# Retention and a squared-ReLU FFN on one core: which engine turns q and k for the later chunks

## The chip, the cores and the metric

The kernel runs on one core of a Trainium2 chip. Time is device time in microseconds from the first to the last instruction of that core; the times of a kernel are from several runs, and the profile is of one execution. Engines are named as in the profile: PE is TensorE (matmul), PEld its weight loads, DVE is VectorE, ACT is ScalarE, POOL is GpSimd, SP is SyncE, which here starts the DMA transfers.

## The reference

A retention layer (attention without softmax, with a decay for each head) feeds a feed-forward network. Shapes: q, k and v are 8 batches x 8 heads x 576 positions x 64; the FFN sees 4608 tokens of width 512, with a hidden width of 2048. All data are float32.

```python
scores = scale * np.matmul(q, k.transpose(0, 1, 3, 2))
Dmat = np.where(rel >= 0, gamma[:, None, None] ** rel[None, :, :], 0.0)
x = np.matmul(scores * Dmat, v)            # then heads side by side: 4608 x 512
h = np.maximum(x @ w_in, 0.0)
out = h * h @ w_out
```

What matters here: the scores contract over the 64 channels of a head, so TensorE needs q and k with the channels on the partitions. They arrive with the positions on the partitions. So each chunk of q and k has to be turned first.

## The kernel before

**Tiling.** The positions of each batch are cut into chunks of 128, the fifth of a batch having 64: 40 chunks, 8 of them short (numbers 4, 9, 14, ..., 39). The tokens are also cut into 9 blocks of 512 for the FFN. Both FFN products are done in a Strassen-like scheme with seven block products in place of eight (`PRODUCTS`), whose sums and differences are made by VectorE.

**First stage, to about 540 us.** A loop over i from 0 to 40 (`N_CH`) does chunk i's scores and finishes chunk i-1, and between these pieces works off FFN steps of earlier blocks. The order is written out by hand; each engine executes its own instructions strictly as listed, and semaphores tie the engines together. One round of the loop, for i above 4, is:

- `retain_a(i-1)`: products within the second half of the chunk (L457) and the growth of the state `u` (L460), then a ScalarE copy of the state (L466);
- `turn(i)` for i below `N_TURN` = 9;
- `move(C, i)`: the copies still open for chunk i;
- `ffn(i-1, 0)`: some FFN steps (`ffn_in`, L616), two or three in most rounds, by the schedule `PACE`; ahead of each step up to three open copies (`move(3)`);
- `retain_b(i-1)`: products with the state (L492), and a ScalarE copy of two columns (L495) that the next products wait for;
- `scores(i)`: the score matmuls (L435), then VectorE multiplies by the mask (L443);
- `retain_c(i-1)`: products within the first half, and the copy out to the FFN's input (L514);
- `spread(i+1)` and `flip(i+2)` for chunks from 9 on, then `ffn(i-1, 1)`, then the loads of later chunks.

**Two ways to turn a chunk.** `turn` uses TensorE: 16 transposes of 64 rows (8 for a short chunk) against an identity (L414) into PSUM, then ScalarE copies out k (L417) and VectorE q (L418). The tile they write in PSUM (`ps_t`, one buffer) is the one that the scores use as well. `flip` uses VectorE: two instructions (L392) that transpose 32x32 blocks of k and of q. The blocks then still lie in the wrong partitions, and `spread` lists 16 copies (8 for a short chunk) that bring them to their places; ScalarE makes these copies (L403, in `move`), a few at a time between the FFN steps.

**An FFN step** is four matmuls (eight records in the profile, L616) into one of three PSUM buffers (h_a, h_b, h_c), and what takes the result out: ScalarE for the first and fourth of the seven products (L626, L632), VectorE for the others (L628, L630, L635, L639, L642), VectorE again for the squares (L623) and for the sums that go to DRAM (L554 to L557). From block 3 on (earlier for a few steps) each step also brings a piece of the second weight's conversion: L210 to L228 and the sums L245 to L248 on VectorE, L218 and L219 on ScalarE.

**Second stage, from about 600 us.** The second FFN product (L903) with all its operands prepared; neither `turn` nor `flip` has a part in it.

**Buffers that matter.** q has three load buffers, k five, v four; the tile for turned q and k has three; the flipped tile two.

Of the kernel before, what the change touches and what calls it, by code (L numbers as in the profile page):

```python
# [40 lines left out]
def kernel(  # L41
# [50 lines left out]
    N_CH = len(chunks)  # L92
# [192 lines left out]
    def fetch_raw(count):  # L285

        for _ in range(count):
            if n_raw[0] < min(N_W1, n_made[0] + N_RAW):
                fetch_w(n_raw[0])
                n_raw[0] += 1  # L290
# [25 lines left out]
    def convert(count):  # L316
        for _ in range(count):
            f = next(w_in_steps, None)
            f and f()
# [52 lines left out]
    def scale_q(i, engine):  # L372
        ci, cs = chunks[i][1], chunks[i][3]
        t = loaded[i][0][:cs]
        engine.tensor_tensor(t, t, dv[:cs, :, NCH + ci:NCH + ci + 1].to_broadcast([cs, H, D]), op=ALU.mult)  # L375
# [1 line left out]

    N_TURN = 9  # L380
    moves = []

    def new_qk(i):
# [16 lines left out]
    def move(count, i=N_CH):  # L400

        while moves and count and moves[0][0] <= i:
            nc.scalar.copy(*moves.pop(0)[1:])  # L403
            count -= 1
# [63 lines left out]
    def retain_a(i):  # L468

        b_, ci, c0, cs = chunks[i]  # L470
        xp[0] = ps_x.tile([128, 2, 256], F32, tag="x", name="x_ps", padded_shape=[128, 2, 512])
        clean.clear()
        if ci == 0:
            u_ps[0] = ps_u.tile([128, HP, D], F32, tag="u", name="u_ps")
        if cs < C:
            return
        own, grow = within(i, 1)
        for j in range(0, len(own), 2):
            for f in own[j:j + 2] + grow[j:j + 2]:
                f()  # L480
        grown(i, 0)

    def retain_b(i):

        s = st[i]
        b_, ci, c0, cs = chunks[i]
        for h in reversed(range(cs // CH)):
            if 2 * ci + h == 0:
                continue
            u = u_sb[(2 * ci + h) % 3]  # L490
            for hp, e, b in HEADS[0:2] + HEADS[4:6] + HEADS[2:4] + HEADS[6:8]:
                nc.tensor.matmul(x_at(hp, b, h), lhsT=u[rows(e), hp, :], rhs=s["qT"][rows(e), hp, CH * h:CH * h + CH],  # L492
                                 start=clears(b, hp // 2), stop=False, skip_group_check=True)

        nc.scalar.copy(u_sb[(2 * ci + (cs // CH)) % 3][:, 0:2, 0:1], xp[0][:, :, cs - CH:cs - CH + 1])  # L495

    def retain_c(i):

        b_, ci, c0, cs = chunks[i]
        own, grow = within(i, 0)  # L500
        more = ci + 1 < NCH
        for j in range(0, len(own), 2):
            for f in own[j:j + 2] + (grow[j:j + 2] if more else []):
                f()
        tok = b_ * S + c0
        at = tok
        p = xp[0][:, :, 0:256].rearrange("p a (g t) -> p a g t", g=2)
        while at < tok + cs:
            n = at // TOK

            while steps and steps[0][0] <= (n - 2 if n > 4 else n - 3):
                step()
            end = min(tok + cs, (n + 1) * TOK)
            nc.scalar.copy(xT[n][:, :, at - n * TOK:end - n * TOK].rearrange("p (a g) t -> p a g t", a=2),  # L514
                           p[:, :, :, at - tok:end - tok])
            if more and at == tok:
                grown(i, 1)
            at = end
            if n_next[0] < N_BLK and (n_next[0] + 1) * TOK <= at:
                steps.extend(block_steps(n_next[0]))  # L520
                n_next[0] += 1
        st[i] = loaded[i] = None
# [47 lines left out]
    def first_in(j, halves=(0, 1)):  # L570

        assert n_made[0] > j
        wi, m, e = pieces[j]
        mp, mm = divmod(m, 2)
        p = ps_f.tile([128, 2, HT], F32, tag="f", name="h_ps")
        w = w_in[mp][:, mm, 2 * e:2 * e + 2, :, :].rearrange("p s c f -> p (s c) f")
        lo, hi = halves[0], halves[-1] + 1
        p = p[:, lo:hi, :]
        for c in range(N_DM):
            nc.tensor.matmul(p.rearrange("p h t -> p (h t)"), lhsT=w[:, c, :], rhs=xT[0][:, c, lo * HT:hi * HT],  # L580
                             start=(c == 0), stop=(c == N_DM - 1))

        t = g_room[mp % 2][:, 3:7:3, mm, :] if e else g_room[mp % 2][:, 0:5:4, mm, :]
        t = t[:, lo:hi, :]
        nc.scalar.activation(t, p, AF.Relu)

        some(2)
        queue.append(lambda: nc.vector.tensor_tensor(t, t, t, op=ALU.mult))
        if mm and e and hi == 2:
            queue.append(lambda: [nc.sync.dma_start(  # L590
                g_dram[0, a:b, :, 2 * mp:2 * mp + 2, :].rearrange("s p m t -> p s (m t)"),
                g_room[mp % 2][:, a:b, :, :].rearrange("p s m t -> p s (m t)")) for a, b in QUARTERS])
        if j >= N_W1 - 4:

            sums_w.setdefault(0, sum_w_in(0)).pop(0)()
            if n_next[0] > 1:
                if 1 not in sums_x:
                    sums_x[1] = sum_x(1)
                sums_x[1].pop(0)()
# [80 lines left out]
    def step():  # L680
        n, f, *args = steps.pop(0)
        done[0] += 1
        f(*args)
# [43 lines left out]
    def warm(count, wide):  # L727
        t = ps_f.tile([128, 512], F32, tag="f", name="idle_ps")
        for _ in range(count):
            if wide:  # L730
                nc.tensor.matmul(t[:, 0:128], lhsT=idle, rhs=idle, start=True, stop=True)
            else:
                for b in range(2):
                    nc.tensor.matmul(t[rows(b), 0:64], lhsT=idle[rows(0), rows(b)], rhs=idle[rows(0), 0:64], start=True, stop=True,
                                     skip_group_check=True)
# [4 lines left out]
    for i in range(N_CH + 1):  # L740
        if i <= N_EARLY:

            if i == 1:
                convert(2)
            elif i == 2:
                convert(5)
            if i >= 1:
                retain_a(i - 1)
                if i < 3:
                    warm(4, False)  # L750
                else:
                    convert(1)
                    first_in(2 * i - 5, (0,))
                    convert(5)
                retain_b(i - 1)
                if i < 3:
                    warm(4, False)
                retain_c(i - 1)
            convert((0, 1, 1, 0, 1)[i])
            if i == N_EARLY:  # L760
                fetch_raw(2)
                step()
            scores(i)
            if i == 2:
                convert(5)
                first_in(0, (0,))
            elif i == 3:
                convert(1)
                first_in(2, (0,))
                convert(5)  # L770
            elif i == N_EARLY:
                convert(5)
                step()
                convert(6)
            scale_q(i + 1, nc.gpsimd)
            if i < N_EARLY:
                if i < 2:
                    warm(6, False)
                turn(i + 1)
        else:  # L780
            if i == N_EARLY + 1:
                gone[0] = TOK
            retain_a(i - 1)
            if i < N_TURN:
                turn(i)
            move(C, i)
            ffn(i - 1, 0)
            retain_b(i - 1)
            if i < N_CH:
                scores(i)  # L790
            retain_c(i - 1)
            if N_TURN <= i + 1 < N_CH:
                spread(i + 1)
            if N_TURN <= i + 2 < N_CH:
                flip(i + 2)
            ffn(i - 1, 1)
        if i == 0:
            fetch_raw(2)
        if i < N_TURN - 1:
            load(i + 3)  # L800
        else:
            if i == N_TURN - 1:
                load(i + 3, "qk")
            if i + 4 < N_CH:
                load(i + 4, "qk")
            if i + 3 < N_CH:
                load(i + 3, "v")
        if 0 < i < N_EARLY:
            fetch_raw(1)
        if i > N_EARLY:  # L810
            for j in range(i + 1 + 2 * (i > N_EARLY + 1), min(i + 4, N_CH)):
                scale_q(j, nc.gpsimd)
# [233 lines left out]
```

## Time and profile before

| | before |
|---|---|
| time, median of 3 runs | 997.35 us (994.88 to 998.98) |
| profiled execution | 996.09 us, span 994.4 us, mean granted TensorE clock 0.993 |
| TensorE busy from 225 to 545 us | 305.9 of 320 us |
| VectorE busy from 225 to 545 us | 286.9 of 320 us |
| ScalarE busy from 225 to 545 us | 186.5 of 320 us |
| copies L403, whole run | 440, 177.0 us busy, 402 ns each |
| flips L392, long chunks, whole run | 24 of k at 699 ns, 24 of q at 665 ns |
| transposes L414, whole run | 68 of k, 68 of q, chunks 0 to 8 |

The busy shares of an engine tell which is fullest, not what the others cost. To see that, one looks at the times when the fullest engine waits, and at what it waits for: the profile lists for each wait the engine and line that ended it. A row of the list of waits reads "who, which tile, which line <- whom it waited for: microseconds in total, times, the longest". The granted clock has to be read beside the busy time: a matmul at half the clock counts as busy for twice as long.

### The profile page before, as it was taken

How to read it: one execution, taken by the hardware profiler on the slowest of the kernel's cores; microseconds unless marked ns; L12 is line 12 of the kernel's file. 1: busy time of each engine (PE TensorE's matmuls, PEld its weight loads, DVE VectorE, ACT ScalarE, POOL GpSimd, SP SyncE). 2: the span in 40 equal slices, each digit the busy share in tenths (PEclk: the TensorE clock that was granted, in tenths of full speed). 3: DMA queues.
4: the chain of work that ended last, by engine and by line, in shares of the span. 5: the costliest groups of instructions: out<-in, count | busy, mean ns of one | idle time of the engine just before them, and what ended most of it. 6: DMA issues, size and time to landing. Idle time of an engine off the chain costs nothing. (4 is left out here: it accounts for less than half of the span.)

```text
span 994.4 us, 24115 instructions
## 1 busy us (share of the span) xinstructions
PE 960.5 (97%) x10092; PEld 855.8 (86%) x10092; DVE 788.7 (79%) x1458; ACT 350.2 (35%) x871; POOL 131.9 (13%) x121
## 2 busy tenths in 40 slices
PE   7899999999999989989999999999999999999998
PEld 6655777888878778877788889999999999999998
DVE  4789798768889899998986777777777677777766
ACT  3445575765665756746651000000000000000000
POOL 3211222212223231312211000000000000000000
PEclk9999999999999999989999999999999999999999
DMA  8884657655697589769358999684673757556351
GB/s 199 245 239 114 184 171 207 191 146 181 204 303 231 172 251 257 218 185 301 109 200 303 402 401 336 233 280 174 234 263 141 274 191 269 192 218 215 125 212 44
DMA packets 185037, 219.19 MB, mean 220 GB/s; under 512 B 118624, under 2 KB 135008, under 8 KB 175968
## 3 DMA queue, kind: packets, MB, share of 16 engines
q1 hardware_dynamic: 182816, 217.13, 67.3%
q8 instruction: 79, 1.29, 0.5%
q10 hardware_dynamic: 2112, 0.52, 0.2%
q14 instruction: 30, 0.25, 0.1%
HBM read 128.23 MB, written 89.39 MB: 219 GB/s over the span
## 5 line engine op out<-in xcount | busy, mean ns | idle before, releaser
L616 PE MATMUL h_b<-room,w 128*128 128x256 f32 x736 | 181.9, 391 | 10.6 <-DVE room L635 4.3
L403 ACT COPY qk<-flip 32x256 f32<-32x256 f32 x440 | 177.0, 402 | 6.3
L616 PEld LDWEIGHTS h_b<-room,w 128*128 128x128 f32 x736 | 139.9, 193 | 33.2 <-DVE room L635 6.1
L903 PE MATMUL o_b<-w,room 128*128 128x128 f32 x1168 | 144.5, 275 | 0.7 <-DVE room L854 0.7
L903 PEld LDWEIGHTS o_b<-w,room 128*128 128x128 f32 x1168 | 137.2, 192 | 0.9 <-DVE room L854 0.9
L903 PE MATMUL o_c<-w,room 128*128 128x128 f32 x1008 | 123.0, 275 | 0.0
L903 PEld LDWEIGHTS o_c<-w,room 128*128 128x128 f32 x1008 | 117.7, 192 | 0.0
L616 PE MATMUL h_c<-room,w 128*128 128x256 f32 x480 | 115.9, 385 | 0.0
L917 ACT COPY r<-o_a 128x128 f32<-128x128 f32 x53 | 14.1, 266 | 272.5 <-PE o_a L903 241.9
L616 PE MATMUL h_a<-room,w 128*128 128x256 f32 x448 | 107.6, 383 | 0.0
L616 PEld LDWEIGHTS h_c<-room,w 128*128 128x128 f32 x480 | 91.9, 193 | 13.6 <-DVE room L642 0.3
L616 PEld LDWEIGHTS h_a<-room,w 128*128 128x128 f32 x448 | 83.7, 190 | 12.1 <-ACT room L626 0.3
L633 POOL TENSOR_TENSOR room<-room 128x512 f32<-128x512 f32 x32 | 36.9, 1152 | 370.4 <-ACT room L632 264.5
L903 PE MATMUL o_a<-w,a 128*128 128x128 f32 x688 | 85.6, 275 | 0.0
L903 PEld LDWEIGHTS o_a<-w,a 128*128 128x128 f32 x688 | 81.2, 192 | 0.1
L623 DVE SCALAR_TENSOR_TENSOR room<-room 128x512 f32<-128x512 f32 x96 | 72.3, 753 | 3.3
L580 PE MATMUL h_ps<-room,w 128*128 128x512 f32 (+1 forms) x160 | 58.7, 515 | 3.3 <-DVE w L228 2.5
L375 POOL TENSOR_TENSOR q_ld<-q_ld,dv 128x512 f32<-128x512 f32 (+1 forms) x39 | 48.6, 1245 | 76.7 <-DMA q_ld<-in_q_dram 50.6
L457 PEld LDWEIGHTS x_ps<-qk,v_ld 64*64 64x64 f32 x1152 | 40.3, 136 | 17.8 <-issue 11.8
L457 PE MATMUL x_ps<-qk,v_ld 64*64 64x64 f32 x1152 | 49.7, 226 | 5.0 <-ACT u_sb L495 4.0
L580 PEld LDWEIGHTS h_ps<-room,w 128*128 128x128 f32 x160 | 29.2, 190 | 25.0 <-issue 20.4
L445 POOL TENSOR_TENSOR v_ld<-v_ld,dv 128x512 f32<-128x512 f32 (+1 forms) x40 | 47.5, 1187 | 13.6 <-DMA v_ld<-in_v_dram 5.9
(111 smaller groups left out, 1392.6 us busy)
## 6 DMA issues: line engine op xcount, KB each, us to landing
g_dram<-room SPq DMA_DIRECT2D x32, 1792.0 KB, 7.7
a<-g_dram SPq DMA_DIRECT2D x43, 1024.0 KB, 7.0
room<-g_dram SPq DMA_DIRECT2D x20, 1024.0 KB, 6.6
w<-w_dram SPq DMA_DIRECT2D x7, 1792.0 KB, 13.2
out_dram<-room SPq DMA_DIRECT2D x17, 512.0 KB, 3.2
w<-in_moe_w_in_dram SPq DMA_DIRECT2D x16, 512.0 KB, 5.6
w<-in_moe_w_out_dram SPq DMA_DIRECT2D x16, 512.0 KB, 3.9
v_ld<-in_v_dram SPq DMA_DIRECT2D x31, 256.0 KB, 4.4
```

What stands on the lines that cost most here:

```text
L375: engine.tensor_tensor(t, t, dv[:cs, :, NCH + ci:NCH + ci + 1].to_broadcast([cs, H, D]), op=ALU.mult)
L403: nc.scalar.copy(*moves.pop(0)[1:])
L445: nc.gpsimd.tensor_tensor(vs[:cs], vs[:cs], dv[:cs, :, ci:ci + 1].to_broadcast([cs, H, D]), op=ALU.mult)
L457: own.append(lambda hp=hp, e=e, b=b: nc.tensor.matmul(x_at(hp, b, h), lhsT=s["vs"][rows(h), 2 * hp + b, :], rhs=s["ret"][rows(h), e, hp, : ...
L580: nc.tensor.matmul(p.rearrange("p h t -> p (h t)"), lhsT=w[:, c, :], rhs=xT[0][:, c, lo * HT:hi * HT], start=(c == 0), stop=(c == N_DM - 1))
L616: nc.tensor.matmul(p[:, mm, :], lhsT=w[:, c, :], rhs=xs[n][right][:, c, :], start=(j in OPENS and mm == 0 and c == 0), stop=(j in CLOSES a ...
L623: nc.vector.scalar_tensor_tensor(t, t, 0.0, t, op0=ALU.max, op1=ALU.mult)
L633: nc.gpsimd.tensor_tensor(g["A11"], g["A11"], g["A11"], op=ALU.mult)
L903: nc.tensor.matmul(p, lhsT=s["lefts"][left][:, m, :], rhs=w_out[j][:, m, WO_SLOT[right], :], start=(i in OPENS and m == 0), stop=(i in CLO ...
L917: nc.scalar.copy(r[:, 0, 0:128], p)
```

## The change

For chunks 19 to 39 TensorE turns q and k again, as it does for chunks 0 to 8; only chunks 9 to 18 keep the way over VectorE and ScalarE. It is meant for the part of the run in which VectorE has the second weight to convert beside the FFN.

```diff
-    N_TURN = 9
+    N_TURN, N_BACK = 9, 19
...
             retain_a(i - 1)
-            if i < N_TURN:
+            if i < N_TURN or N_BACK <= i < N_CH:
                 turn(i)
             move(C, i)
             ffn(i - 1, 0)
...
             retain_c(i - 1)
-            if N_TURN <= i + 1 < N_CH:
+            if N_TURN <= i + 1 < N_BACK:
                 spread(i + 1)
-            if N_TURN <= i + 2 < N_CH:
+            if N_TURN <= i + 2 < N_BACK:
                 flip(i + 2)
             ffn(i - 1, 1)
```

The loads, and the order of the instructions on SyncE and GpSimd, stay as they are.

## The prediction

> **What bounds the kernel now.** I read first the busy shares and the 40 slices of the page, then the busy time of each engine in stretches of 10 us, then the list of who waited for whom on TensorE from 225 to 541 us, then the order of time around the longest of these waits. The busy shares say that TensorE (97%) is the engine that sets the time and that VectorE (79%) and ScalarE (35%) are not:
>
> ```profile
> PE 960.5 (97%) x10092; PEld 855.8 (86%) x10092; DVE 788.7 (79%) x1458; ACT 350.2 (35%) x871; POOL 131.9 (13%) x121
> PEclk9999999999999999989999999999999999999999
> ```
>
> The average hides the stage that the change touches: chunks 19 to 39, from the first flip that goes (210.9 us) to the last scores (528 us). There the other two are nearly as full. Columns of the stretches: from and to, length, then busy us of PE, PEld, DVE, ACT and POOL with instruction counts, granted clock, DMA share, GB/s:
>
> ```profile
> 245.00:255.00 10.00, 9.19 (x94) 7.65 (x94) 9.90 (x18) 6.59 (x16) 0.47 (x1) 1.00 0.42 105
> 255.00:265.00 10.00, 10.00 (x77) 8.23 (x73) 7.45 (x13) 6.30 (x16) 3.84 (x4) 0.83 0.90 281
> ...
> 315.00:325.00 10.00, 8.53 (x90) 7.08 (x86) 9.15 (x16) 9.06 (x21) 3.68 (x4) 1.00 0.95 265
> ...
> 425.00:435.00 10.00, 6.52 (x50) 5.05 (x49) 9.96 (x15) 3.85 (x10) 3.60 (x3) 0.73 0.06 25
> ```
>
> Read the last row: TensorE worked 6.5 of 10 us, at a mean clock of 0.73, while VectorE worked all ten. So TensorE is the bound, but in a few places it stands still for VectorE or ScalarE. All its waits from 225 to 541 us (columns: total us, times, longest):
>
> ```profile
> PE sc_ps L435 <- ACT qk L403: 3.5, 6, 1.1
> PE h_b L616 <- DVE room L628: 3.5, 1, 3.5
> PE x_ps L457 <- ACT u_sb L495: 2.8, 3, 2.1
> PE h_b L616 <- DVE room L635: 2.6, 2, 1.3
> PE h_b L616 <- DVE room L541: 1.6, 1, 1.6
> ```
>
> That is 14.0 us. Two more losses don't show as waits. First, three times a set of score matmuls that takes 0.65 us elsewhere is stretched (252.55 to 254.57, 322.91 to 325.85, 464.47 to 466.93 us, 7.4 us in place of 1.95): 5.5 us, of which 3.5 are in the list, so 1.9 more. Second, the granted clock falls to 0.50 after such places: the stretches at 255, 425, 435 and 495 us show 0.83, 0.73, 0.93 and 0.83, that is 1.7 + 2.7 + 0.7 + 1.7 = 6.8 us, less 0.6 that fell into the wait itself: 6.2 us. All told about **22 us** of TensorE's time in this stage are lost, and every one of these waits is for an instruction of VectorE or ScalarE.
>
> **What the skill says.** "TensorE: Matmul & The Clock Gate", Part 1 (the HAM clock gate): after a window of about 3.4 us with too little activity the clock is halved, and it comes back after a busy window. The trace agrees: 0.50 from about 430 to 436.6 us, behind a wait of 3.48 us, and about 3.4 us at half clock behind the stretched scores at 253 us. Part 4 of the page (PE-mode transpose) says that a transpose does not count as activity there. No run so far tells; but in the early stage, where TensorE already turns q and k, the clock is 1.00 from 0 to 100 us. "PSUM — Partial Sum Buffer", Terms, says that two engines must not be on one bank and quadrant at once. It bears on the two copies out of the turned chunk, which share their banks; in the program order the VectorE copy (L418) waits for the ScalarE copy (L417), and the trace has that wait: 4.8 us in 3 times.
>
> **The change part by part.** 21 chunks move: 16 of 128 rows, and 5 of 64 rows (19, 24, 29, 34, 39).
>
> (a) Removed from ScalarE: 16x16 + 5x8 = 296 copies (L403). The trace has just these 296 between 225 and 541 us, 119.1 us at 402 ns. Added: 21 copies L417, 16 of 585 ns and 5 of 372 ns, 11.2 us. ScalarE is lighter by 108 us. Its time is worth only what TensorE waited for: the three stretched scores (5.5 us), and the clock dip behind the first (1.7 us).
>
> (b) Removed from VectorE: 21 pairs of L392, 16x(699+665) + 5x(693+659) ns = 28.6 us. Added: 21 copies L418, 16x685 + 5x419 ns = 13.1 us. VectorE is lighter by 15.5 us, 0.68 us a chunk.
>
> (c) Added on TensorE: 16 transposes for a long chunk, 8 for a short one. The early turns price it in place: x8 and x8 from 62.42 to the next work at 63.06, and a short chunk, x4 and x4, from 34.44 to 35.08, 0.64 us each, since the two halves of a long chunk run beside one another:
>
> ```profile
> 62.42 0.46 PE L414 MATMUL t_ps<-w,k_ld 64*128 64x64 f32 x8
> 62.72 0.41 PE L414 MATMUL t_ps<-w,q_ld 64*128 64x64 f32 x8
> 63.06 3.70 PE L580 MATMUL h_ps<-room,w 128*128 128x512 f32 x8
> ```
>
> 21 x 0.64 = **13.4 us**, all on the engine that sets the end. By the mean durations (257 and 245 ns, start included) with no overlap of halves it could be up to about 20 us (9.1 us busy for the 136 early ones, 67 ns each, times 296 = 19.8); I take 13.4, since those sums hold the start of the kernel.
>
> (d) The waits for VectorE (7.7 us: 1.60, 1.28, 1.29 and 3.48). In each the VectorE has been full for some 10 us (9.9 of 10), so work taken from it there shortens the wait: 0.68 us a chunk net, and TensorE, coming 0.64 us later because it transposes, would wait that much less. That is 1.3 us for each: 1.3 + 1.28 + 1.29 gone. In the run-up to the longest the flips at 425.5 and 426.1 us go (1.28 with their overlap) and no added copy stands between, so 1.9 of 3.48: 5.8 us in all. The dip behind it (2.8 us) I count half, since 1.6 us of wait beside small matmuls may still trigger it: 1.4.
>
> (e) The wait for L495 (2.14 of its 2.8 us at 496.8 us). ScalarE had finished its copies and stood in L218, which waited for VectorE (L210, 1.01 us). So it is VectorE's lateness again; 0.68 + 0.64 = 1.3 us goes, with ScalarE free of copies also in the short ones 0.6: 2.0, and its dip, 1.7.
>
> (f) New waits. L418 must be through before the scores. Ahead of it on VectorE stand only evacuations of the earlier FFN steps; behind it the evacuations of the half chunk's FFN steps, for whose banks TensorE could wait. Between turn and scores TensorE has two or three FFN steps of 1.73 us and 0.4 to 0.7 us of L492, about 5 to 6 us. VectorE's lag, read as the time from the end of the scores to the start of L443, is 0 to 4.1 us and once 5.6 (chunk 32). L443 has the same room on the other side of the scores and was waited for 0.8 us in the whole run. So I cost L418 at nothing, hidden behind these steps. Early on TensorE did wait for it, 2.4 us in 2 times; there only one FFN step lies between.
>
> (g) Loads of q. Three buffers turn around at the transposes in place of the flips, two chunks later. The q load of chunk i+4 is then held until turn(i+1), soon after it is reached; the queue was held there anyway by L558, which waited 148 us for VectorE between 200 and 620 us. The data are needed two chunks (of some 14 us) later than for the flip, against 5.7 us for a landing. Nothing.
>
> The sum: 13.4 - (5.5 + 1.7 + 5.8 + 1.4 + 2.0 + 1.7) = 13.4 - 18.1 = -4.7 us. It reaches the end: from 540 to 600 us TensorE is 100% busy and from 530 on it waits 1.1 us in all. 997.35 - 4.7 = **992.6**.
>
> **The rivals.** *Everything comes back*: with both engines lighter all 22.1 us go: 13.4 - 22.1 = -8.7, 988.6 us. For it: all losses hang on the two relieved engines. Against: VectorE still works 0.85 of this stage (286.9 of 320 us from 225 us on, less 15.5). *TensorE pays, VectorE stays late*: the bursts of weight work (L245 to L248 and slow two-operand adds of 1.2 to 1.5 us at 351 and 416 us) make the waits, not the flips; then only ScalarE's 7.2 us come back: +6.2, 1003.5 us. For it: TensorE is the fullest engine and gets the work. *The copy takes the place of the wait*: L418 waits for L417 and holds up VectorE, and TensorE waits as it did early, 1.2 us at each of half the chunks, 13 us, on top of -4.7: +8, 1005.6 us, slower. Against it: the room in (f).
>
> **How the numbers follow.** Forecast 0.60, spread 989.5 to 996, half of it beyond 0.5% (992.4); everything back 0.16; TensorE pays 0.16; the copy 0.08. Faster 0.46, same 0.30, slower 0.24. The range takes in the floor, 988, and reaches up to the third case, 1003.
>
> **What would show it.** The waits of scores for L403 after 225 us are gone; L414 costs 0.64 us a chunk; TensorE's idle time from 225 to 541 us falls from 14 to about 4 us and the clock in the 10 us stretches stays at 1.00 but for one or so; ScalarE loses 108 us, VectorE 15.5. It is wrong if L435 waits for L418 or L417 at many chunks, if L628 and L635 keep their waits, if the transposes cost over 0.9 us in place, or if the clock falls at other places.

## The result and the profile after

The changed kernel takes 991.97 us (median of 4 runs, 991.45 to 993.54) against 996.61 us of the kernel before in the same job, that is, among runs of both taken together (994.88 to 998.98): a ratio of 0.9954, 95% interval 0.993 to 0.9979. In a later job it took 992.71 us against 996.19, a ratio of 0.9966 (0.9952 to 0.998). So it is 3.5 to 4.6 us faster.

The busy shares and the clock in the 40 slices, after:

```profile
PE 968.1 (98%) x10388; PEld 864.0 (87%) x10388; DVE 769.7 (78%) x1437; ACT 242.6 (24%) x596; POOL 126.9 (13%) x121
PEclk9999999999999999999999999999999999999999
```

TensorE is busier (7.6 us more), ScalarE has lost 107.6 us, VectorE 19.0. That TensorE's busy time rises by less than the 13.4 us of the transposes fits the clock: the 8 in the row of before is gone, and the same products take less time (before, an FFN step at half clock took 3.78 us at 431 us, one at full clock 1.89 us at 437 us). All waits of TensorE from 225 to 541 us, after (total us, times, longest):

```profile
PE x_ps L457 <- ACT u_sb L495: 1.4, 2, 1.0
PE h_b L616 <- DVE room L541: 1.0, 1, 1.0
PE sc_ps L435 <- DVE qk L418: 0.7, 1, 0.7
PE h_b L616 <- DVE room L635: 0.6, 1, 0.6
```

14.0 us have become 3.7; the waits for L403 and L628 are gone. Three of the stretches of 10 us that were shown of before (length, then busy us of PE, PEld, DVE, ACT, POOL, granted clock, DMA share, GB/s):

```profile
245.00:255.00 10.00, 10.00 (x60) 8.57 (x59) 9.64 (x16) 2.98 (x6) 0.74 (x1) 1.00 0.45 160
255.00:265.00 10.00, 9.98 (x145) 8.30 (x144) 8.12 (x13) 1.98 (x5) 4.37 (x4) 1.00 0.87 281
...
425.00:435.00 10.00, 9.84 (x87) 8.08 (x85) 9.93 (x16) 1.92 (x4) 4.31 (x3) 1.00 0.39 144
```

TensorE is full in them, and the clock is 1.00 in every stretch from 225 to 545 us. VectorE is still full in the last one, but TensorE now waits for it only 0.6 us near there, and no clock dip (a stretch at half clock) follows.

One thing changed there that the edit doesn't touch. Ahead of the longest wait of before (3.48 us, up to 431.01) VectorE made two additions of the weight conversion, L247 and L248, while GpSimd was at work. Before, then after:

```profile
427.67 1.21 POOL L633 TENSOR_TENSOR room<-room 128x512 f32<-128x512 f32 x1 [8.48 <-ACT room L632]
427.90 1.25 DVE L247 TENSOR_TENSOR w<-w,w 128x256 f32<-128x256 f32 x1
428.84 1.23 POOL L375 TENSOR_TENSOR q_ld<-q_ld,dv 128x512 f32<-128x512 f32 x1
429.19 1.17 DVE L248 TENSOR_TENSOR w<-w,w 128x256 f32<-128x256 f32 x1
430.28 0.68 DVE L628 TENSOR_TENSOR room<-h_b,room 128x512 f32<-128x512 f32 x1
```

```profile
427.40 0.42 DVE L247 TENSOR_TENSOR w<-w,w 128x256 f32<-128x256 f32 x1
427.86 0.42 DVE L248 TENSOR_TENSOR w<-w,w 128x256 f32<-128x256 f32 x1
428.20 0.69 DVE L628 TENSOR_TENSOR room<-h_b,room 128x512 f32<-128x512 f32 x1
430.69 1.50 POOL L633 TENSOR_TENSOR room<-room 128x512 f32<-128x512 f32 x1 [12.04 <-ACT room L632]
```

The two additions took 2.42 us before and 0.84 after, when GpSimd began later. From 205 to 540 us, 30 instructions of VectorE were over 0.1 us longer before than the median of their line and shape, by 18.6 us in all; after, it was 15, by 8.6 us. GpSimd was at work during at least a third of each. The prediction names such slow additions only in a rival and has no term for their getting shorter. Three of the four waits for VectorE before (at 355.6, 372.2 and 431.0 us) have 1.1 to 2.3 us of such lengthening in the 10 us ahead of them. No run took work off GpSimd, so how much of the gain hangs on it stays open.

One execution differs from another by up to 4 us in its first 200 us, which the change doesn't touch. So I compare the **stage**: from the first scores of chunk 17 to those of chunk 39. In the order of time, before and then after:

```profile
209.49 0.65 PE L435 MATMUL sc_ps<-qk 64*64 64x64 f32 x32
527.42 0.65 PE L435 MATMUL sc_ps<-qk 64*64 64x64 f32 x16
```

```profile
211.80 0.65 PE L435 MATMUL sc_ps<-qk 64*64 64x64 f32 x32
525.32 0.65 PE L435 MATMUL sc_ps<-qk 64*64 64x64 f32 x16
```

The stage takes 317.93 us before and 313.52 after, 4.41 less; a second profile of the changed kernel gave 313.52 again. The rest of the run, from there to the end, is nearly the same (467.0 and 466.5 us).

The clock differs between executions too. The 29 of before in the later job had mean granted clocks of 0.988 to 0.998 (median 0.993), the nine of the changed kernel 0.993 to 1.000 (median 1.000). The three dips of the profile alone make 0.993, so not every execution of before has all of them. The four at 0.997 or 0.998 took 993.29 to 994.21 us, only 0.6 to 1.5 us more than the changed kernel's median. This points to the clock for most of the gain.

### The profile page after: what moved, and what is told of

It is laid out like the page before. It is cut to its first block, busy times and chain, and to the rows that moved or that the text cites. A ratio compares the mean times of both kernels' runs of the same rounds, so it can differ in the third digit from the quotient of the medians.

```text
span 991.8 us, 24367 instructions
## 1 busy us (share of the span) xinstructions
PE 968.1 (98%) x10388; PEld 864.0 (87%) x10388; DVE 769.7 (78%) x1437; ACT 242.6 (24%) x596; POOL 126.9 (13%) x121
## 4 chain that ended last, share of the span: by engine, by line
PE 86%; DVE 8%; ACT 2%; SPq 1%; issue 1%; DMA 1%; DVEq 0%; ACTq 0%
PE o_b L903 17%; PE h_b L616 15%; PE o_c L903 11%; PE o_a L903 11%; PE h_c L616 10%; PE h_a L616 10%; PE h_ps L580 3%; PE x_ps L457 3%; PE sc_ps L435 2%; PE x_ps L492 2%; PE t_ps L414 1%; DVE w L222 1%; DVE w L225 1%; DVE room L623 1%; SPq L151 1%
## 5 line engine op out<-in xcount | busy, mean ns | idle before, releaser
L616 PE MATMUL h_b<-room,w 128*128 128x256 f32 x736 | 177.1, 384 | 4.5 <-DVE room L635 2.3
L616 PEld LDWEIGHTS h_b<-room,w 128*128 128x128 f32 x736 | 137.3, 190 | 25.4 <-DVE room L635 3.5
L616 PE MATMUL h_a<-room,w 128*128 128x256 f32 x448 | 107.6, 383 | 0.0
L616 PEld LDWEIGHTS h_a<-room,w 128*128 128x128 f32 x448 | 83.8, 190 | 11.8
L633 POOL TENSOR_TENSOR room<-room 128x512 f32<-128x512 f32 x32 | 36.0, 1126 | 367.9 <-ACT room L632 280.4
L623 DVE SCALAR_TENSOR_TENSOR room<-room 128x512 f32<-128x512 f32 x96 | 70.4, 733 | 3.3
L403 ACT COPY qk<-flip 32x256 f32<-32x256 f32 x144 | 57.9, 402 | 2.1
L375 POOL TENSOR_TENSOR q_ld<-q_ld,dv 128x512 f32<-128x512 f32 (+1 forms) x39 | 45.8, 1173 | 81.6 <-DMA q_ld<-in_q_dram 78.5
L635 DVE TENSOR_TENSOR room<-h_b,room 128x512 f32<-128x512 f32 x32 | 22.0, 688 | 41.6 <-PE h_b L616 41.6
L457 PEld LDWEIGHTS x_ps<-qk,v_ld 64*64 64x64 f32 x1152 | 40.3, 136 | 15.7 <-issue 10.5
L457 PE MATMUL x_ps<-qk,v_ld 64*64 64x64 f32 x1152 | 49.7, 226 | 3.1 <-ACT u_sb L495 2.2
```

Of the source, the lines that this page charges most:

```text
L457: own.append(lambda hp=hp, e=e, b=b: nc.tensor.matmul(x_at(hp, b, h), lhsT=s["vs"][rows(h), 2 * hp + b, :], rhs=s["ret"][rows(h), e, hp, : ...
L616: nc.tensor.matmul(p[:, mm, :], lhsT=w[:, c, :], rhs=xs[n][right][:, c, :], start=(j in OPENS and mm == 0 and c == 0), stop=(j in CLOSES a ...
L623: nc.vector.scalar_tensor_tensor(t, t, 0.0, t, op0=ALU.max, op1=ALU.mult)
L633: nc.gpsimd.tensor_tensor(g["A11"], g["A11"], g["A11"], op=ALU.mult)
L635: nc.vector.tensor_tensor(g["A22"], p, p15, op=ALU.add)
```

## The experiments

"Stage" is measured as above; medians are to be compared with before in the same job. Stages are from one profile of each kernel, and one dip of 3.41 us at half clock makes 1.7 us of a stage. A line of dots in a diff stands for lines left out.

| kernel | median us | before, same job | ratio, 95% interval | stage us |
|---|---|---|---|---|
| changed | 991.97 | 996.61 | 0.9954 (0.993 to 0.9979) | 313.52 |
| no_flips | 987.79 | 997.60 | 0.9898 (0.9876 to 0.992) | 305.83 |
| no_copies | 988.83 | 997.60 | 0.9907 (0.9891 to 0.9923) | 307.74 |
| neither | 981.19 | 997.60 | 0.9833 (0.9812 to 0.9853) | 300.17 |
| turn_twice | 1001.45 | 997.60 | 1.0038 (1.0025 to 1.005) | 321.76 |
| back9 | 997.27 | 997.39 | 1.0003 (0.9989 to 1.0016) | 313.97 |
| back24 | 991.57 | 997.39 | 0.9939 (0.9916 to 0.9961) | 311.99 |
| act_both | 990.65 | 997.39 | 0.9931 (0.991 to 0.9953) | 311.05 |
| after_short | 994.62 | 997.39 | 0.9972 (0.996 to 0.9984) | 315.08 |
| after_again | 992.71 | 996.19 | 0.9966 (0.9952 to 0.998) | 313.52 |
| act24 | 989.23 | 996.19 | 0.9931 (0.9909 to 0.9952) | 309.77 |
| picked | 986.53 | 996.19 | 0.9903 (0.9884 to 0.9922) | 307.46 |
| picked_vec | 992.70 | 996.19 | 0.9966 (0.9957 to 0.9976) | 314.22 |

### VectorE's share: no_flips

```diff
-            if N_TURN <= i + 2 < N_CH:
+            if N_TURN <= i + 2 < N_BACK:
                 flip(i + 2)
+            elif N_BACK <= i + 2 < N_CH:
+                st[i + 2]["flip"] = flipped[0]
...
```

`N_BACK` is 19, and `flipped[0]` is the tile of the last chunk that was flipped, chunk 18.

> The kernel before, with the flips of chunks 19 to 39 left out (28.6 us of VectorE); the copies stay and take the flipped tile of chunk 18, so these chunks compute with wrong q and k. No work is added on TensorE. Theory (both engines' load makes TensorE's waits): the waits for L628, L635, L541 and the late L495, with the clock dips behind them, go, 10.9 us by the prediction's terms and up to 14 since more than the net 15.5 us is taken away; the waits of the scores for L403 stay at some 3.5 us. 10 to 14 us faster than before. Rival (the bursts of weight work on VectorE make the waits, not the flips): 0 to 3 us faster, L628 and L635 keep their waits.

9.8 us faster, just under the 10 to 14 expected, and 12.1 in the stage. TensorE's waits from 205 to 545 us in this kernel, whose line numbers are here two above those of before (L437 is the scores, L405 the copy, L497 is L495, L543 is L541, L637 is L635):

```profile
PE sc_ps L437 <- ACT qk L405: 2.9, 4, 1.2
PE x_ps L459 <- ACT u_sb L497: 1.8, 3, 1.2
PE h_b L618 <- DVE room L543: 1.6, 1, 1.6
PE h_b L618 <- DVE room L637: 1.5, 1, 1.5
PE h_c L618 <- DVE room L632: 0.6, 1, 0.6
```

As the theory had it, the scores still wait for the copies, and the long wait of before (L628, 3.48 us) is gone with its clock dip: every stretch is at 1.00. The rival that only bursts of weight work matter is out, though they have a part in it: L247 and L248, which took 2.42 us ahead of the long wait, belong to them. And not all waits for VectorE go: 3.7 us stay.

### ScalarE's share: no_copies

```diff
-    lhsT=kT[rows(e), hp, t], rhs=qT[rows(e), hp, t],
+    lhsT=kT[rows(e), hp, t] if i < N_BACK else msk[rows(e), 0, 0, :],
+    rhs=qT[rows(e), hp, t] if i < N_BACK else msk[rows(e), 0, 0, :],
...
-            if N_TURN <= i + 1 < N_CH:
+            if N_TURN <= i + 1 < N_BACK:
                 spread(i + 1)
+            elif N_BACK <= i + 1 < N_CH:
+                new_qk(i + 1)
```

> The kernel before, with the ScalarE copies of chunks 19 to 39 left out (119 us of ScalarE); the flips stay, and the score and state products of these chunks take a constant in place of q and k. Theory: the stretched scores (5.5 us) and the dip behind the first (1.7 us) go, with some short waits for L495 (0.6 us): 7 to 8 us faster than before; the waits for L628, L635 and L541 stay. Rival (ScalarE at 60% was never the cause, it only waits for VectorE too): 0 to 2 us faster.

8.8 us faster, 10.2 in the stage: more than ScalarE's direct waits are worth. The waits of TensorE (numbers one above, L629 is L628):

```profile
PE x_ps L458 <- ACT u_sb L496: 3.2, 2, 2.8
PE h_b L617 <- DVE room L636: 2.8, 3, 1.6
PE h_b L617 <- DVE room L542: 1.6, 1, 1.6
PE h_b L617 <- DVE room L629: 1.1, 1, 1.1
PE h_c L617 <- DVE room L631: 0.9, 1, 0.9
```

The wait for L628 has shrunk from 3.5 to 1.1 us although VectorE does the same work as before. Of these 2.4 us, 1.6 are L247 and L248: they took 0.41 and 0.42 us here, since both had begun (423.40 and 423.85 us) when GpSimd began its L633 (423.99). With it the long dip went, and the one behind the scores; only one is left, of 3.41 us from 489.25 on, behind the 2.8 us for L495. That gives back 4.5 of the clock's 6.2 us. In the kernel before VectorE also waits for ScalarE's part of the weight conversion, here in the list of VectorE's waits from 205 to 545 us:

```profile
DVE w L222 <- ACT w L219: 2.4, 1, 2.4
```

It is gone without the copies, and in the changed kernel. But it ends at 336.5 us, 95 us ahead of the long wait, and without the flips it is there with the same 2.4 us while the long wait is gone. So it is not what makes the long wait. What the trace shows is that leaving out ScalarE's copies moved, at this place, which instructions of VectorE and GpSimd fell together; how much of the 10.2 us that is, no run tells apart.

### Both, and nothing in their place: neither

The two edits together.

> Flips and copies of chunks 19 to 39 both left out, nothing in their place; the score and state products take a constant. Theory: nearly all of the 22 us come back, 973 to 978 us; then the changed kernel stands 13.4 us (the transposes) and some 2 us (what its copies bring) above it. Rival (the transposes cost more in place than 0.64 us a chunk): the changed kernel stands 20 us or more above it. Rival (VectorE's weight work makes most waits): only 7 to 10 us come back, 987 to 990 us, and the transposes would then be nearly free.

16.4 us faster and 17.8 in the stage; the two parts alone give 12.1 + 10.2 = 22.3, so they overlap. 981 us is above the 973 to 978 expected, and below the rival's 987: 5.1 us of waits stay, 1.7 for L635, 1.6 for L541, 1.4 for L495 and 0.4 for L443. All but the 1.4 are for VectorE's other work.

In the second stage one more wait of 1.4 us stands at its start (for L857, here the first sums of the second product), which the kernels with a later start don't have to that size: 0.7 us before. The changed kernel's stage is 313.52 - 300.17 = **13.35 us** above this one, by the medians of two jobs 11.8 us, where I had expected 13.4 and some 2. This is all that turning by TensorE brings with it, the copies out and the waits included: TensorE waits 3.7 us in the changed kernel and 5.1 here. That it meets 13.4 so closely is in part luck. The direct reading is the time of each set in the changed kernel: 0.64 or 0.65 us from its start to the next work in 20 of the 21, 0.71 in one that a wait follows, 13.5 us in all.

### The price of a set of transposes: turn_twice

```diff
-        for j in (1, 0):
+        for j in (1, 0) * (2 if i >= N_BACK else 1):
```

> The changed kernel, with the transposes of chunks 19 to 39 made twice into the same place. Theory: 0.64 us of TensorE a chunk, nearly all on the path: 12 to 13.4 us slower than the changed kernel. Rival (up to 67 ns a transpose): 18 to 20 us slower. Rival (they hide in TensorE's waits): under 6 us slower.

8.2 us more in the stage than the changed kernel, 9.5 by the medians of two jobs: between the theory and the rival that they hide. The order of time shows why:

```profile
250.21 0.46 PE L414 MATMUL t_ps<-w,k_ld 64*128 64x64 f32 x8
250.50 0.41 PE L414 MATMUL t_ps<-w,q_ld 64*128 64x64 f32 x8
250.75 0.41 PE L414 MATMUL t_ps<-w,k_ld 64*128 64x64 f32 x8
251.00 0.41 PE L414 MATMUL t_ps<-w,q_ld 64*128 64x64 f32 x8
251.34 1.99 PE L616 MATMUL h_c<-room,w 128*128 128x256 f32 x8
```

Two sets take 1.13 us, so the second takes 0.49, 0.15 us less than the first; I take the 0.15 for the going over from and to other products, which no run shows by itself. 21 x 0.49 = 10.3, and TensorE, later by so much, waits 1.6 us in place of 3.7: 10.3 - 2.1 = 8.2.

### How far back: back9 and back24

`N_BACK` is 9 (TensorE turns all chunks) or 24.

> TensorE turns every chunk, 9 to 18 too. 10 more sets of transposes, 6.4 us of TensorE. In the kernel before, TensorE waits there, from 97 to 210 us, for VectorE and ScalarE only 4.6 us in all and the clock stays at 1.00. Theory (a set costs 0.64 us and only existing waits come back): 2 to 4 us slower than the changed kernel, 1 to 3 us faster than before. Rival (relief of VectorE and ScalarE is worth the same everywhere, 0.2 us a chunk): 2 us faster than the changed kernel.

> TensorE turns from chunk 24 on only; chunks 19 to 23 go back to VectorE and ScalarE. 3.2 us of TensorE saved; back come the stretched scores at 253 us (1.4 us), the clock dip behind them (1.7) and part of the wait at 296 us (0.6). Theory: within 1.5 us of the changed kernel, 4 to 5 us faster than before. Rival (relief early in the stage is needed for the later waits too): 3 us or more slower than the changed kernel.

back9 loses all of the gain: it is as long as before. From the scores of chunk 5 to those of chunk 17 it takes 160.38 us (54.14 to 214.52) against 155.85 (53.64 to 209.49), 4.5 more; its 6.4 us of transposes bring back only 1.8 us of waits there (from 97 us on: 4.6 before, 2.8 now), and a dip comes that before doesn't have, 125.4 to 128.8 us, 1.7 us: it stands behind a wait of the scores for L418, 1.81 us up to 123.71. So the rival that the copy takes the place of the wait comes true here at one chunk. These make +6.3; the 1.8 us down to the measured 4.5 are mostly not placed. I had expected 2 to 4. back24 is 1.5 us shorter in the stage than the changed kernel, at the edge of what was expected. Its sum was off, though: the stretched scores are back (1.99 us at 254.66), but the dip behind them, for which I had counted 1.7 us, is not. By the medians the two kernels can't be told apart (their intervals overlap), so it stays open whether chunks 19 to 23 are worth their transposes.

### Both copies on ScalarE: act_both and act24

```diff
-        nc.vector.tensor_copy(to[:, 0].rearrange("p d h t -> p h d t"), p[:, :n_h, 0, :, :])
+        if i < N_TURN:
+            nc.vector.tensor_copy(to[:, 0].rearrange("p d h t -> p h d t"), p[:, :n_h, 0, :, :])
+        else:
+            nc.scalar.copy(to[:, 0].rearrange("p d h t -> p h d t"), p[:, :n_h, 0, :, :])
```

(For act24 with `N_BACK` = 24.)

> The changed kernel, with both copies out of a turned chunk on ScalarE for chunks 19 to 39: VectorE loses 13.1 us more, ScalarE gains 11 us. VectorE's 5.8 us of waiting for L417 go too. What is left to win is TensorE's waits for VectorE, 3.7 us in the profile of the changed kernel. Theory (VectorE no longer matters much): 0 to 2 us faster than the changed kernel. Rival (VectorE is still the second limit): 3 us or more faster. Rival (the copies one behind the other on ScalarE come late for the scores): 1 to 3 us slower.

> TensorE turns from chunk 24 on, both copies on ScalarE. The parts add up: from chunk 24 on 1.5 us less in the stage than from 19, both copies on ScalarE some 2 us: 7 to 9 us faster than before. If the waits that come back at chunks 19 to 23 (1.6 us at 296 us, the stretched scores at 253) weigh more than the 3.2 us of transposes, it is no faster than with both copies on ScalarE from 19 on (6.7 us faster than before).

act_both takes 2.5 us off the changed kernel's stage, between the theory and the rival that VectorE is still the second limit; TensorE's waits are down to 1.7 us. The copies one behind the other do no harm. act24 nearly adds up to the parts (4.4 + 1.5 + 2.5): 8.2 us less than before in the stage, 7.0 by the median.

### Only some chunks: after_short, picked, picked_vec

```diff
+    BY_PE = (20, 25, 30, 35)
...
-            if i < N_TURN:
+            if i < N_TURN or i in BY_PE:
                 turn(i)
...
-            if N_TURN <= i + 2 < N_CH:
+            if N_TURN <= i + 2 < N_CH and i + 2 not in BY_PE:
                 flip(i + 2)
```

`spread` is left out for the same chunks. In picked and picked_vec `BY_PE` is (20, 23, 25, 27, 28, 30, 32, 33, 35, 37); picked also makes both copies on ScalarE, as act_both does.

> The kernel before, with TensorE turning only chunks 20, 25, 30 and 35, those behind a short chunk, where the scores were stretched by the copies. 2.6 us of TensorE; back come the stretched scores (5.5 us) and the clock dip (1.7 us), and 2.7 us of VectorE. Theory (the stretched scores come from these four chunks' copies alone): 4 to 6 us faster than before, with a fifth of the transposes as good as the changed kernel. Rival (the whole load of ScalarE matters): the waits for L403 move to other chunks, 0 to 2 us faster.

> The kernel before, with TensorE turning ten chunks only, those just ahead of its waits (20, 23, 25, 27, 28, 30, 32, 33, 35, 37), both copies on ScalarE. 6.4 us of TensorE in place of 13.4. Theory (the waits hang on the chunks near them): 15 to 18 of the 22 us come back, 9 to 11 us faster than before. Rival (VectorE and ScalarE need the relief of all chunks, waits move to the chunks not picked): 5 to 7 us faster, as with both copies on ScalarE for all.

> The same ten chunks, with q copied by VectorE as in the change. VectorE has 6.8 us more. Theory: 1 to 3 us slower than with both copies on ScalarE, 7 to 9 us faster than before.

after_short gained 2.8 us, less than expected. No score waits for L403 any more, but one waits 0.9 us for L418, two waits for L635 of 0.9 and 0.7 us stand where there were none, at 262 and 277 us, and the long wait stays, with its dip (L629 is L628):

```profile
432.58 3.78 PE L617 MATMUL h_b<-room,w 128*128 128x256 f32 x8 [3.62 <-DVE room L629]
```

The wait for L495 at 498.1 us is here 2.14 us too, as long as before (496.8 us), but no dip follows it, where before one did.

picked is the fastest of the kernels that leave no work out, 9.7 us faster than before with 10 sets of transposes in place of 21. picked_vec differs from it by ten copies on VectorE, 6.8 us of work, and is 6.2 us slower; I had expected 1 to 3. Two stretches of picked_vec, and the same of picked (in the last row of numbers, the clock is third from the end):

```profile
435.00:445.00 10.00, 10.00 (x129) 8.35 (x128) 7.72 (x14) 4.72 (x12) 0.00 (x0) 0.86 1.07 303
495.00:505.00 10.00, 9.88 (x95) 8.19 (x96) 7.79 (x13) 5.82 (x17) 2.38 (x2) 0.83 0.50 186
```

```profile
435.00:445.00 10.00, 10.00 (x76) 8.57 (x75) 6.77 (x12) 3.76 (x9) 3.07 (x3) 1.00 1.03 348
495.00:505.00 10.00, 10.00 (x135) 8.67 (x134) 8.62 (x16) 5.82 (x15) 2.33 (x2) 1.00 0.23 85
```

TensorE's waits are 7.7 us against 4.8, and with 0.3 us from 425 on the clock costs 0.3 + 1.4 + 1.7 = 3.4 us against none: 6.3 together. The waits ahead of the dips are 2.14 us (at 433.8) and 2.23 (at 495.1) in picked_vec, 1.54 and 1.64 in picked. So about 0.6 us more of waiting went with the clock's falling here. The length doesn't decide it alone, as the 2.14 us of after_short show.

after_again is the changed kernel once more.

> The changed kernel once more, beside the runs of before that the other three share: 4 to 6 us faster than before.

3.5 us faster than before by the median, a little under the 4 expected; its stage agrees to 0.01 us.

## Why the prediction was right

The forecast of 992.6 us was near the measured 991.97 by way of its terms, with several of them off in size and one missing. That the sum comes so close (-4.7 us against -4.4 in the stage) is in part luck, since they were off to both sides.

- **The price of the transposes** held. In the changed kernel a set runs from 251.77 to the next work at 252.41, 0.64 us, and the 21 make 13.5 us. VectorE lost 19.0 us where I counted 15.5; some of its other instructions run shorter (the 96 of L623 take 733 ns in place of 753), fewer of them beside GpSimd's.

- **What comes back**: 4.4 + 13.4 = 17.8 us of the stage, against 18.1. Term by term: the stretched scores are gone (5.5, as forecast). The waits for VectorE fell by 6.1 us (7.7 to 1.6), forecast 5.8; but L628's went whole, 3.5 in place of 1.9, of which 1.6 are the shorter L247 and L248 that no term had, while L541's fell by 0.6 in place of 1.3 and a new one for L635 of 0.6 came. The waits for L495 fell by 1.4, forecast 2.0. All the clock's 6.2 us came back, where I counted 4.8, with half of the long dip in it: mis-sized, since no wait for L628 was left at that place, where I had worked out 1.6 us. These four make 19.2; less the new wait below it is 18.5, and the 0.7 us to the measured 17.8 are not placed. By this account the stage would have become 1.8 us longer without the clock's 6.2 us: the change pays by the clock.
- **The split between the engines** was under-sized for ScalarE: I gave its copies 7.2 us and the short waits; without them the stage is 10.2 us shorter, because the wait for L628 shrank and its dip went as well. The sum didn't suffer since both were relieved at once.
- **The new wait** for L418, costed at nothing, was 0.7 us in one place (327 us). VectorE's waiting for L417, 5.8 us in 5 times, had a price only in a rival. With it and the copy itself off VectorE (act_both) the stage is 2.5 us shorter: small, but not nothing.
- **The loads of q**: SyncE waits much longer for the transposes than "soon". The longest of its waits in the changed kernel, 225 to 541 us:

```profile
SPq L558 <- DVE room L557: 95.0, 19, 14.6
SPq L149 <- PE t_ps L414: 61.6, 16, 9.9
```

  Yet no wait of TensorE for data appears in the list, so costing it at nothing was right.
- **The rivals.** "TensorE pays, VectorE stays late" fails: leaving out the flips alone brings 12.1 us of the stage back. "The copy takes the place of the wait" needed 13 us of waits for L418, and there are 0.7. "Everything comes back" was 3.7 us of waits away.

On the two statements of the skill: "TensorE: Matmul & The Clock Gate", Part 1, agrees in how long the clock stays halved: each dip of the stage lasted 3.41 or 6.82 us, one or two of its windows. How much activity is too little these runs don't settle: the clock fell behind waits shorter than a window (2.14 and 2.23 us in picked_vec), and behind one of the same 2.14 us in after_short it didn't. Its Part 4, that transposes don't count as activity for the clock, leaves no mark here: the clock stays at 1.00 through the stage even with two sets in a row beside the small products, though these 1.13 us are short beside 3.41. What I read for the early stage says less than I thought: the profile of before records no clock ahead of 16.6 us.

## What to carry to other kernels

An engine that is 97% busy can still be given work where that work takes others out of its way: count what it waits for in that stage, add what the clock loses behind the waits, and set it against the price of the added work in place. Give it the work only where the waits are: with both copies on ScalarE, ten chunks chosen by the list of waits brought 9.7 us and all twenty-one 6.7 (the intervals overlap a little, the stages differ by 3.6 us; ten other chunks were not tried), and turning chunks 9 to 18 by TensorE too, where there was little to win, cost the whole gain of the change. And when a helper engine is the one that is late, look also at which of its instructions took longer there than elsewhere, and at what ran beside them.

## What the runs showed of the hardware

- A wait of TensorE can cost 1.8 times its length: behind 3.48 us of waiting the clock took another 2.8 us, behind 2.14 another 1.7. But the same 2.14 us at the same place cost nothing more in after_short. From 205 to 545 us, in the fourteen profiles, all waits at an FFN product or at L457 that a dip followed were of 2.14 to 3.62 us, and none of 1.66 us or less was followed by one. Of seven score sets stretched by 1.3 to 2.3 us (in before, no_flips, back24 and act24) one was and six were not, so the length alone does not decide it.
- A second set of 16 transposes right behind the first costs 0.49 us, the first 0.64.
- Additions on VectorE took 0.42 us (128x256) or 0.68 us (128x512) with no GpSimd instruction beside them, and up to 1.25 and 1.54 us with one. The instructions that read PSUM (L628 and L635 among them) and the transposes L392 kept their 0.7 us beside GpSimd. Why, no run here shows.
